# Where three pieces of VectorE and TensorE work stand in the second MLP halves of an mLSTM and Fourier-mixing kernel

## The chip, the cores and the metric

One core of a Trainium2 chip runs the whole kernel. The metric is the time of one execution on the device, in microseconds; smaller is better. Five engines run side by side, each through its own stream of instructions in the order in which the program was built: TensorE (PE in the profile, with its weight loads as PEld), VectorE (DVE), ScalarE (ACT), GpSimd (POOL) and SyncE (SP, which only issues transfers here). Products of PE land in the banks of PSUM and are read from there by DVE and ACT.

## The reference

For four batches, an mLSTM cell over 768 tokens and 8 heads of 40 gives x (768 tokens, 320 columns). Then:

```python
X = np.fft.fft(x, axis=1)
X = np.fft.fft(X, axis=2)
mixed = np.real(X).astype(np.float32)
u = x + mixed
mu = np.mean(u, axis=-1, keepdims=True)
var = np.mean((u - mu) ** 2, axis=-1, keepdims=True)
un = (u - mu) / np.sqrt(var + 1e-06)
ch = np.maximum(un @ w_ch1, 0.0) @ w_ch2
return (u + ch).astype(np.float32)
```

`w_ch1` is 320 x 1280 and `w_ch2` is 1280 x 320. Everything here is in fp32.

## The kernel before

**Stages.** Each batch goes through the mLSTM (in chunks of 128 tokens), the mixing (two Fourier transforms as products with tables, `mix_*`), the first MLP half (`mlp_block`, 1280 intermediate columns in ten blocks) and the second half (`mlp_out` for batch 0, `mlp_out_pair` for the others). The stages of different batches overlap: while the second half of batch b runs, the mixing of batch b + 1 is done, and beside batch 1's second half the mLSTM of batch 3 runs as well (beside batch 2's none is left).

**The order** is written out by hand. `at(slot, phase, fn, ...)` (L127) notes a call, and `run` (L130) makes all calls sorted by slot, then phase. The phases are `EVAC, FILL, MAIN, FILL_PE = range(4)` (L136), with fractions between: in a slot, 2.05 stands behind 2.0 and ahead of 2.5 and 2.6. The order of the calls is the order on every engine; nothing is moved later.

**The second half** (`plan_mlp`, L1352; `mlp_out_pair`, L1309). Six token columns of 128 are taken as three pairs n = 0, 1, 2, each with one column of either group. A pair is done by seven products in place of eight, in Strassen's manner: sums S1 to S4 of blocks of the intermediate columns (`hidden_sums`, L1300, one DVE instruction of 128x640 each, line L1307 in the profile; S4 is the tile `s_last`) meet sums T2 to T4 of the weights. Each product is ten matmuls of 160 columns (L1321) into one of two PSUM banks, and each is followed by a `residual` (L1267, instruction at L1271), in which DVE adds the scaled bank to the output column. A pair takes four slots, its steps:

- step 0: two products of plain blocks into banks x and y (four fifths of the first, two fifths of the second, the rest of the first, the rest of the second), and two residuals;
- step 1: S2 with T2 into x, S1 with a weight block into y, and two residuals;
- step 2: S3 with T3 into x, S4 with a weight block into y, two residuals and a store;
- step 3: one plain block with T4 into x, one residual and a store.

Banks x and y change places from one pair to the next. So step 0's first product of a pair needs the bank read by the second residual of step 2 of the pair before, and step 0's second product needs the bank read by its step 3 residual. Within a pair, step 1's first product waits for step 0's first residual, and step 2's first product for step 1's first residual. The sums of the next pair are made in steps 2 (S1, S2) and 3 (S3, S4).

**The mixing beside it** (`plan_mix`, L1062). For batches 2 and 3 it lies in the slots s_mix + 0 to s_mix + 11, which are the twelve slots of batch 1's and batch 2's second half: s_mix + 4 is step 0 of pair 1, s_mix + 8 is step 0 of pair 2. `mix_feat` (L965, L986) multiplies with the feature table into a bank `pu`: 128x161, 128x159 and 128x320, for p = 0, 1, 2. p = 1 and p = 2 use the same bank. `mix_add` (L988) adds `pu` to a token column on DVE: L1008 to L1011 and the statistics L1013 and L1014; for column 4 a copy and a memset (L1003, L1004) come first. The columns are added in the order 0, 5, 1, 4, 2, 3, in the slots s_mix + 4, 4, 5, 6, 8, 9, at phase MAIN + 0.5; columns 2 and 3 read the product p = 2. ScalarE centres a column (L1022, `uc`), PE transposes it (L1033), and ScalarE copies it to `uT` (L1038).

**`mlp_sums`** (L1178, L1183) makes four differences of `uT` on DVE (128x384 each: T3, B12, T2, T4) that the first MLP half of the next batch uses; its first product at step 1 reads B12, and its step 2 uses the bank of the last `residual` of the second half before.

Of the kernel before, what the change touches and what calls it, by code (L numbers as in the profile page):

```python
# [30 lines left out]
TG = NT // 2  # L31
# [26 lines left out]
def kernel(  # L58
# [68 lines left out]
    def at(slot, phase, fn, *args):  # L127
        plan.setdefault((slot, phase), []).append((fn, args))
# [7 lines left out]
    EVAC, FILL, MAIN, FILL_PE = range(4)  # L136
# [925 lines left out]
    def plan_mix(b, s0, x_done, s_feat, s_add, s_turn):  # L1062
        for j in range(TG):
            p = TG - 1 - j
            if b == 0:
                at((17, 18, 18.5)[j], FILL + (0.1, 0.07, 0.3)[j], mix_fold, b, p)
                s, phase = ((17, 3), (19, 3), (22, 4))[j]
                for i, part in enumerate(((0,), (1,)) if j == 1 else ((0, 1),)):
                    at(s, FILL_PE + phase + 0.1 * i, mix_seq, b, p, part)
                at(*((18, FILL_PE + 0.2) if j == 0 else (s, FILL_PE + phase + 0.2)), mix_tail, b, p)  # L1070
            else:
                at(x_done[j] + (b > 1 and j == TG - 1), FILL + 0.5 if b < 2 else FILL_PE + 0.2, mix_fold, b, p)
            if b > 0 and j == 0:
                for step in range(2):
                    at(*((x_done[-1], FILL + 0.55) if b == 1 else (x_done[-1] + 2 + 2 * step, FILL_PE + 0.25)),
                       mix_fold_again, b, step)
                at(s0, FILL_PE + 4, mix_seq, b, p, (0,))
                at(s0 + 1, FILL_PE + 4, mix_seq, b, p, (1,))
                at(s0 + 2, FILL_PE + 4, mix_tail, b, p)
        for i in range(2):  # L1080
            at(s0 + 1 if b == 0 else s0 + 1 + i, FILL, mix_seq_out, b, i)
        at(s0 + (1 if b == 0 else 3), FILL + 0.1, mix_tail_out, b)
        for p in range(TG):
            for i in range(3) if b == 0 and p == TG - 1 else ():
                at(s_feat[p] + i, FILL_PE + 5.1, mix_feat, b, p, slice(i, i + 1))
            if b == 0 and p == TG - 2:
                at(s_feat[p], FILL_PE + 4.06, mix_feat, b, p, slice(0, 3))
                at(s_feat[p] + 3, FILL_PE + 5.05, mix_feat, b, p, slice(3, 5))
            elif b == 0 and p == 0:
                at(s_feat[p], FILL_PE + 4, mix_feat, b, p, slice(0, 2))  # L1090
                at(s_feat[p], FILL_PE + 4.04, mix_feat, b, p, slice(2, 3))
            elif b > 0 or p < TG - 1:
                at(s_feat[p], FILL_PE + 4, mix_feat, b, p)
        for c, a, t in zip(ORDER, s_add, s_turn):
            at(a, FILL if b < 2 else MAIN + 0.5, mix_add, b, c)
            at(*(((32, EVAC + 0.1) if c == 3 else (a, FILL + 0.25) if c in (4, 2) else (t, FILL + 0.1)) if b == 0 else
                 (t, FILL + 0.1)), mix_center, b, c)
            at(t, FILL_PE + (5 if b == 0 or c in ORDER[:4] else -0.1), mix_turn, b, c)
            if b > 0:
                at(t, FILL_PE + 6, mix_turn_out, b, c)  # L1100
            elif t < s_mlp:
                at(t + 1, FILL + 0.2, mix_turn_out, b, c)
            else:
                at(t + 1, EVAC, mix_turn_out, b, c)
# [247 lines left out]
    def plan_mlp(b, s):  # L1352
        groups = range(NT // TG)
        for i in range(NFF // 2) if b > 0 else ():
            for step in range(4):
                at(s, MAIN, mlp_block, b, i, step)
                s += 1
            end = i == NFF // 2 - 1
            for n, (gr, f) in enumerate(((1, 2 * i + 1), (1, 2 * i), (0, 2 * i))):
                at(*((s - 1, MAIN + (-0.1 if gr else 0.1)) if end else (s + n, MAIN + 0.5)), mlp_relu_in_place, gr, f)  # L1360
        for gr, n in IN_ORDER if b == 0 else ():
            for f in (2 * n, 2 * n + 1):
                at(s, MAIN, mlp_in, b, gr, f)
                s += 1
            i = IN_ORDER.index((gr, n))
            if i < 4 or i % 2 == 0:
                at(*((s, MAIN + 0.5) if i == 1 else (s - 1, MAIN + (-0.1 if i == 2 else 0.2))), mlp_in_rests, b, i, False)
                if i > 3:
                    at(s - 1, MAIN + 0.25, mlp_in_rests, b, i + 1, True)
            for f in (2 * n, 2 * n + 1):  # L1370
                at(s + (i == 1), EVAC, mlp_relu, b, gr, f)
        if b > 0:
            for j in range(1, 5):
                at(s - (5, 4, 3, 3)[j - 1], FILL_PE + 0.3, hidden_sums, 0, (j,), 0, NFF // 2 - 2)
            at(s, EVAC, hidden_sums, 0, (1, 2), NFF // 2 - 2, NFF // 2)
            at(s, MAIN + 0.1, hidden_sums, 0, (3, 4), NFF // 2 - 2, NFF // 2)
        for n in range(TG) if b > 0 else ():
            for step in range(4):
                at(s, MAIN, mlp_out_pair, b, n, step)
                if n < TG - 1 and step > 1:  # L1380
                    for j in (2 * step - 3, 2 * step - 2):
                        at(s, MAIN + 0.6, hidden_sums, n + 1, (j,))
                s += 1
        for gr in groups if b == 0 else ():
            for i in range(TG):
                for half in range(2):
                    at(s, MAIN, mlp_out, b, gr, i, half)
                    s += 1
                n = gr * TG + i
                at(*((s + 2, MAIN + 0.1) if n == 0 else (s + 1, EVAC) if n == 1 else (s, EVAC)), mlp_store, b, gr, i)  # L1390
# [11 lines left out]
    def plan_batch(b, s_mlstm, s_mix, s_mlp):  # L1402
        if b == 0:
            plan_mlstm(b)
        else:
            plan_halves(b, s_mlstm)
        done = [s_mlstm + n for n in ((17, 19, 22) if b == 0 else (14, 17, 20))]
        assert s_mix >= done[-1] and s_mlp >= s_mix + 9
        late = [s_mlp + 2 * c for c in range(TG)]
        if b == 0:  # L1410
            feat = [s_mix + 1, s_mix + 1, s_mix + 2]
            turn = [s_mix + 2, s_mix + 3, s_mix + 4]
            add = turn + [s_mix + 5, s_mix + 6, s_mix + 7]
            late = [s_mlp, s_mlp + 1, s_mlp + 2]
        else:
            feat = [s_mix + c for c in ((3, 4, 6) if b == 1 else (3, 4, 7))]
            add = [s_mix + c for c in ((4, 4, 5, 6, 7, 7) if b == 1 else (4, 4, 5, 6, 8, 9))]
            turn = [s_mix + c for c in ((5, 6, 6) if b == 1 else (6, 7, 8))]
            late = [s_mix + c for c in ((7, 8, 8) if b == 1 else (9, 10, 10))]
            at(s_mlp, EVAC + 0.5, mlp_sums)  # L1420
        plan_mix(b, s_mix, done, feat, add, turn + late)
        s = s_mlp + NFF + 2
        at(s, FILL + 0.6, mix_rstd, b)
        for n in range(3):
            at(48 + n if b == 0 else s, FILL + 0.65, mix_rstd_step, b)
        plan_mlp(b, s_mlp)

    s_mlp = 31
    plan_batch(0, 0, 22, s_mlp)
    plan_batch(1, 32, 54, s_mlp + MLP_SLOTS)  # L1430
    plan_batch(2, 54, 83, s_mlp + 2 * MLP_SLOTS)
    plan_batch(3, 86, 115, s_mlp + 3 * MLP_SLOTS)
    for n in range(4):
# [181 lines left out]
```

## Time and profile before

| | us |
|---|---|
| median of 3 runs | 393.28 |
| lowest, highest | 390.28, 393.6 |
| the profiled execution | 390.56 |
| its span, first to last instruction | 388.8 |
| second half of batch 1, with the mixing of batch 2 | 197.7 to 244.1 |
| second half of batch 2, with the mixing of batch 3 | 284.4 to 324.2 |

The profile gives the busy time of each engine, and for each instruction that found its engine idle the wait and what ended it. A row of the timeline is: start in us from the first instruction, duration in us, engine, line of the kernel, operation, output<-inputs, shape, count, and in brackets the idle time ahead of it with its releaser. Ends of matmuls are modelled, so a row's duration overlaps the next row's start; the distance from start to start is the pace of PE. The token columns of all batches are named x in the trace; which batch is meant follows from the place.

### The profile page before, as it was taken

What the parts mean: (1) busy time and instruction counts of PE and PEld (TensorE: products, weight loads), DVE (VectorE), ACT (ScalarE), POOL (GpSimd) and SP (SyncE); (2) the same over time, 40 slices, a digit from 0 to 9 for tenths busy, and PEclk for the clock granted to TensorE, in tenths of its full rate; (3) what the DMA queues carried; (4) which work ended last, traced back from release to release, by engine and by line L of the source; (5) the groups of instructions that cost most, each with busy time, mean ns of one, the idle gap of its engine ahead of it and who ended that gap; (6) DMA issues with size and microseconds to landing.
All of it is one profiled execution on the core that took longest, in us unless ns stands there. A gap on an engine that the chain in (4) does not pass through costs nothing.

```text
span 388.8 us, 11401 instructions
## 1 busy us (share of the span) xinstructions
PE 375.2 (96%) x4598; PEld 274.1 (70%) x4598; DVE 282.4 (73%) x668; ACT 175.4 (45%) x505; POOL 132.3 (34%) x238
## 2 busy tenths in 40 slices
PE   8999888999999999999999999999999999999996
PEld 6887455666567777565578989565588996546996
DVE  8798898799997596786965786876755785246651
ACT  5988766868342233654553052663530133545000
POOL 5665434866685122561601433651300000020000
PEclk9999999999999999999999999999999999999999
DMA  7979489699971243464003644700001000000010
GB/s 203 293 211 322 134 232 265 177 276 260 233 191 36 88 140 110 143 179 121 0 3 90 155 117 114 195 21 3 0 0 35 5 31 34 2 0 2 35 35 34
DMA packets 21617, 43.99 MB, mean 113 GB/s; under 512 B 3493, under 2 KB 9853, under 8 KB 21437
## 3 DMA queue, kind: packets, MB, share of 16 engines
q1 hardware_dynamic: 21564, 43.27, 38.7%
q8 instruction: 36, 0.59, 0.7%
q14 instruction: 17, 0.13, 0.1%
HBM read 39.16 MB, written 4.10 MB: 111 GB/s over the span
## 4 chain that ended last, share of the span: by engine, by line
PE 74%; DVE 17%; issue 3%; ACT 1%; POOL 0%; DVEq 0%; ACTq 0%; POOLq 0%
PE po L1321 21%; PE pm L1195 16%; PE po L1265 8%; PE pm L1112 7%; PE pm L1129 4%; PE ph L581 4%; PE ps L581 4%; PE pu L986 3%; DVE so L771 2%; PE pz L940 2%; DVE x L758 1%; PE hb L581 1%; PE put L1033 1%; PE pzt L940 1%; DVE fe L878 1%
## 5 line engine op out<-in xcount | busy, mean ns | idle before, releaser
L1271 DVE SCALAR_TENSOR_TENSOR x<-po,rstd,x 128x160 f32<-128x160 f32 (+1 forms) x69 | 27.2, 394 | 38.3 <-PE po L1321 35.9
L1201 DVE TENSOR_TENSOR h<-h,pm 128x384 f32<-128x384 f32 x60 | 30.5, 550 | 27.0 <-PE pm L1112 12.6
L577 POOL TENSOR_SCALAR_AFFINE_SELECT W<-W 64x512 f32<-64x512 f32 x36 | 28.3, 786 | 32.5 <-ACT W L550 31.2
L704 POOL TENSOR_TENSOR C<-C,decB 128x164 f32<-128x164 f32 x33 | 18.4, 559 | 59.4 <-DVE C L711 58.0
L1195 PE MATMUL pm<-uT,w_sb 128*128 128x384 f32 x90 | 37.8, 507 | 0.4 <-DVE uT L1183 0.2
L550 ACT ACTIVATE W<-W,colT 128x64 f32<-128x64 f32 x144 | 36.7, 337 | 0.0
L1265 PE MATMUL po<-w_sb,h 128*128 128x320 f32 x120 | 33.9, 433 | 0.0
L1112 PE MATMUL pm<-uT,w_sb 64*64 64x384 f32 x320 | 33.3, 497 | 0.0
L1057 POOL TENSOR_TENSOR t<-rstd 128x6 f32<-128x6 f32 x12 | 3.5, 292 | 80.4 <-DVE v L1051 79.9
L562 POOL TENSOR_TENSOR qg<-qk,Gb 128x512 f32<-128x512 f32 x21 | 27.0, 1284 | 10.5 <-DMA qk<-in_qkT 10.2
L1321 PE MATMUL po<-T,S 128*128 128x160 f32 x180 | 27.9, 302 | 1.1 <-DVE x L1271 1.1
L1265 PEld LDWEIGHTS po<-w_sb,h 128*128 128x128 f32 x120 | 22.4, 190 | 9.1 <-issue 0.3
L1129 PE MATMUL pm<-uT,w_sb 128*128 128x384 f32 x80 | 28.5, 496 | 0.0
L1321 PEld LDWEIGHTS po<-T,S 128*128 128x128 f32 x180 | 25.4, 190 | 2.4 <-DVE x L1271 1.5
L1321 PE MATMUL po<-w_sb,h 128*128 128x160 f32 x180 | 26.3, 300 | 0.0
L1321 PEld LDWEIGHTS po<-w_sb,h 128*128 128x128 f32 x180 | 25.2, 190 | 1.5 <-DVE x L1271 0.3
L1195 PEld LDWEIGHTS pm<-uT,w_sb 128*128 128x128 f32 x90 | 15.4, 189 | 14.7 <-DVE h L1201 6.7
L1248 ACT ACTIVATE h<-h 128x384 f32<-128x384 f32 x45 | 23.1, 520 | 2.9 <-DVE h L1201 2.9
L1112 PEld LDWEIGHTS pm<-uT,w_sb 64*64 64x64 f32 x320 | 11.3, 132 | 18.1 <-issue 14.9
L1022 ACT ACTIVATE uc<-x 128x384 f32<-128x384 f32 x24 | 14.5, 615 | 19.9 <-DVE x L1014 19.9
L1038 ACT COPY uT<-put 128x384 f32<-128x384 f32 x21 | 9.6, 478 | 26.9 <-PE put L1033 26.8
L568 POOL TENSOR_TENSOR vw<-kvt,colT 128x328 f32<-128x328 f32 x23 | 20.0, 869 | 4.0 <-issue 2.2
(255 smaller groups left out, 833.2 us busy)
## 6 DMA issues: line engine op xcount, KB each, us to landing
kvt<-in_kv SPq DMA_DIRECT2D x24, 336.0 KB
qk<-in_qkT SPq DMA_DIRECT2D x48, 160.0 KB
raw<-in_w SPq DMA_DIRECT2D x10, 640.0 KB
Gb<-G_d SPq DMA_DIRECT2D x42, 128.0 KB
W<-M_d SPq DMA_DIRECT2D x36, 128.0 KB
so<-in_o SPq DMA_DIRECT2D x24, 160.0 KB
out<-x SPq DMA_DIRECT2D x24, 160.0 KB
ds_sb<-in_dft_s SPq DMA_DIRECT2D x1, 1158.0 KB
```

Of the source, the lines that this page charges most:

```text
L550: nc.scalar.activation(out=k.W[:, h, :], in_=M, func=AF.Exp, scale=-1.0, bias=colT[:, c, 0, b * H + h:b * H + h + 1])
L562: nc.gpsimd.tensor_tensor(out=k.qg[:, :, t], in0=k.qk[:, 0, :, t], in1=k.Gb[:, :, t], op=OP.mult)
L577: nc.gpsimd.affine_select(out=W, in_=W, compare_op=OP.is_ge, fill=0.0, base=base, pattern=[[0, H], [-1 if back else 1, LH]], channel_multi ...
L581: nc.tensor.matmul(out, w, x, start=start, stop=True, skip_group_check=True)
L1112: nc.tensor.matmul(banks[i][half(cols)], w1_rest(n)[half(i), half(cols)], u[half(i)], start=start, stop=not start, skip_group_check=True)
L1129: nc.tensor.matmul(k.pm[i], w1_block(ch, f // 2 * 2 + i), u[2 * ch], start=(ch == 0 and not ahead), stop=(ch == 1 and (ahead or n == 2)), ...
L1195: nc.tensor.matmul(bank, w, u, start=start, stop=True, skip_group_check=True)
L1201: nc.vector.tensor_tensor(out=h, in0=h, in1=bank, op=OP.add)
L1248: nc.scalar.activation(out=h, in_=h, func=AF.Relu, scale=-1.0)
L1265: nc.tensor.matmul(k.po[m], hidden(gr, f)[:, i * L:(i + 1) * L], w2_sb[:, f, :], start=(f == 0), stop=(f == NFF - 1))
L1271: nc.vector.scalar_tensor_tensor(out=u, in0=po, scalar=k.rstd[:, c:c + 1], in1=u, op0=OP.mult, op1=OP.add)
L1321: nc.tensor.matmul(po, a[:, f], w[:, f], start=start and f == 0, stop=f == half - 1, skip_group_check=True)
```

## The change

Three calls are put at other places; no instruction is added, removed or altered.

- `hidden_sums` for the next pair: S3 and S4 go from the slot of step 3 to the slot after it, that is step 0 of the next pair, at the same phase MAIN + 0.6. S1 and S2 stay. This concerns batches 1, 2 and 3, pairs 1 and 2.
- `mix_feat` with p = 2, for batches 2 and 3: from slot s_mix + 7, phase FILL_PE + 4 (behind step 3 of pair 1) to slot s_mix + 8, phase MAIN + 0.05 (behind the products of step 0 of pair 2).
- `mlp_sums` for batches 2 and 3: from the first slot of the next first half to the slot before it, phase MAIN - 0.05, that is ahead of step 3 of pair 2 with its residual. Batch 1 keeps its place.

```diff
@@ plan_mix
             elif b == 0 and p == 0:
                 at(s_feat[p], FILL_PE + 4, mix_feat, b, p, slice(0, 2))
                 at(s_feat[p], FILL_PE + 4.04, mix_feat, b, p, slice(2, 3))
+            elif b > 1 and p == TG - 1:
+                at(s_feat[p] + 1, MAIN + 0.05, mix_feat, b, p)
             elif b > 0 or p < TG - 1:
                 at(s_feat[p], FILL_PE + 4, mix_feat, b, p)
@@ plan_mlp
                 at(s, MAIN, mlp_out_pair, b, n, step)
                 if n < TG - 1 and step > 1:
                     for j in (2 * step - 3, 2 * step - 2):
-                        at(s, MAIN + 0.6, hidden_sums, n + 1, (j,))
+                        at(s + 1 if j > 2 else s, MAIN + 0.6, hidden_sums, n + 1, (j,))
                 s += 1
@@ plan_batch
-            at(s_mlp, EVAC + 0.5, mlp_sums)
+            at(*((s_mlp, EVAC + 0.5) if b == 1 else (s_mlp - 1, MAIN - 0.05)), mlp_sums)
```

In the built streams the change moves instructions on two engines: on DVE the sums, the adds around them and the four differences, on PE the three products of `mix_feat`. The streams of ACT, POOL and SP are the same as before.

## The prediction

> **What bounds the kernel now.** The page first: TensorE (PE) is busy 96% of the span at the full granted clock, so only its own idle time can be won and whatever makes it wait costs in full.
>
> ```profile
> span 388.8 us, 11401 instructions
> ...
> PE 375.2 (96%) x4598; PEld 274.1 (70%) x4598; DVE 282.4 (73%) x668; ACT 175.4 (45%) x505; POOL 132.3 (34%) x238
> ...
> PEclk9999999999999999999999999999999999999999
> ```
>
> Next the waits of PE between 198 and 327 us, which hold the output halves of batches 1 and 2 (197.7 to 244.1 and 284.4 to 324.2; batch 3's ends the span). All three name VectorE (DVE):
>
> ```profile
> PE po L1321 <- DVE x L1271: 1.1, 1, 1.1
> PE pu L986 <- DVE x L1011: 0.4, 1, 0.4
> PE pm L1195 <- DVE uT L1183: 0.2, 1, 0.2
> ```
>
> Then the timeline there (start us, us, engine, line). Batch 1, pairs 1 and 2:
>
> ```profile
> 212.48 0.81 DVE L1307 TENSOR_TENSOR S<-h,h 128x640 f32<-128x640 f32 x1
> 213.21 0.82 DVE L1307 TENSOR_TENSOR s_last<-h,S 128x640 f32<-128x640 f32 x1
> ...
> 216.43 0.39 DVE L1271 SCALAR_TENSOR_TENSOR x<-po,rstd,x 128x160 f32<-128x160 f32 x1 [1.57 <-PE po L1321]
> ...
> 220.85 0.29 DVE L711 TENSOR_TENSOR C<-C,ps 128x164 f32<-128x164 f32 x1
> 221.06 0.38 DVE L1271 SCALAR_TENSOR_TENSOR x<-po,rstd,x 128x160 f32<-128x160 f32 x1
> ...
> 221.49 1.63 PE L1321 MATMUL po<-T,S 128*128 128x160 f32 x10
> ...
> 233.30 0.87 DVE L1271 SCALAR_TENSOR_TENSOR x<-po,rstd,x 128x160 f32<-128x160 f32 x2
> ...
> 233.73 1.62 PE L1321 MATMUL po<-T,S 128*128 128x160 f32 x10 [1.08 <-DVE x L1271]
> ```
>
> Batch 2, the same places, and its hand-off to batch 3's first half:
>
> ```profile
> 306.25 0.35 DVE L1271 SCALAR_TENSOR_TENSOR x<-po,rstd,x 128x160 f32<-128x160 f32 x1
> ...
> 306.79 1.52 PE L1321 MATMUL po<-T,S 128*128 128x160 f32 x10
> ...
> 311.80 0.78 PE L986 MATMUL pu<-dd_sb,Z 128*128 128x161 f32 x4 [0.44 <-DVE x L1011]
> ...
> 313.89 0.38 DVE L1271 SCALAR_TENSOR_TENSOR x<-po,rstd,x 128x160 f32<-128x160 f32 x1
> ...
> 325.86 0.91 PE L1195 MATMUL pm<-uT,w_sb 128*128 128x384 f32 x2 [0.24 <-DVE uT L1183]
> ```
>
> See in it: pair 1's S3 and S4 (212.48, 213.21) stand ahead of a 1.57 us hole in DVE: free. From 217 on DVE runs two token adds back to back, and the residual that frees PE's bank ends at 221.44, 0.05 before PE restarts; in batch 2 it ends 306.60, 0.19 before. There DVE has nothing to spare.
>
> **Units from rows.** Ten 160-column matmuls (one product) take 1.36 (379.93 to 381.29), the feature product 1.09 (228.03 to 229.12), three transposes 0.33 (309.51 to 309.84), a 384-column matmul 0.32 (324.16 to 325.45 for four). A restart after a wait costs 0.10 more (221.49 to 222.95 is 1.46). On DVE, start to next start: S3 0.73, S4 0.73, S1 with S2 1.58, residual 0.30, token add 1.66, column 4's add 2.31, one `mlp_sums` subtraction 0.59. A residual starts 0.20 after its product; PE follows 0.05 after a residual.
>
> **Part 1: S3, S4 of the next pair one slot later.** Six moves, two DVE instructions each; no DMA, and the built streams of PE, ACT, POOL and SP keep their order here. They leave the place before step 0's residuals and come behind them, but at phase 2.6, that is behind the token adds at 2.5, and ahead of step 1's residuals.
>
> *Pair 1, batch 1.* The adds still start at 217.54, since they follow a residual that PE paces. S3 starts at 220.85, S4 at 221.58, L711 at 222.31, step 1's first residual at 222.52 instead of 221.06; PE restarts at 222.95 instead of 221.49: +1.46. Queued behind the sums: both residuals of step 1, the add of column 1, all that follows. *Pair 1, batch 2.* The residual goes from 306.25 to 307.71, PE from 306.79 to about 308.13, plus a restart: +1.43. Bounds: the hole they leave gives nothing back (DVE waits there for PE), so no gain; lower 1.26 (1.46 less the 0.19 of slack) per batch, upper 1.96 (two at 0.98, the slowest row of these sums); I take the 0.73 pitch, since POOL does nothing there in batch 2 and little in batch 1.
>
> *Batch 3, no adds between.* S3 and S4 make step 0's first residual late twice now (PE resumes at 368.64 and 378.47 with 0.13 lost each). Behind step 0 they start at 378.9, step 1's residual ends 380.8, PE needs it at 381.2: hidden, slack 0.4. -0.26.
>
> **Part 2: feature product p=2 behind step 0 of pair 2** (with pair 2's S3, S4 behind the add of column 2). Now it stands between step 3 and step 0 of pair 2, and its 1.09 us cover a DVE chain: last residual of step 2, add of column 4, S1, S2, then step 3's residual, which frees the bank of step 0's second product.
>
> *Batch 1.* PE's step 2 ends at 224.41; that residual ends 229.91, and PE gets to the product at 230.53: slack 0.62. Without the feature product PE comes 1.09 earlier and waits 0.52 with the latency, +0.10. In exchange S3, S4 no longer stand (231.58 to 233.07) ahead of step 0's first residual: transposes at 232.16 end 232.49 but PE went on at 233.73; 1.24 and a restart go, -1.34. The later sums start after the column 2 add and are done before PE, busy 2.7 us with attention products, wants step 1's residual. Sum: 0.62 - 1.34 = -0.72.
>
> *Batch 2.* No attention work lies between. The stall at 311.80 goes (0.60 past the pace, as the product before began at 309.84; with 0.08 and 0.05 of slow matmuls behind it, 0.73), but PE then meets the bank at 312.62 on the old clock, while the chain frees it at 314.32 as before: step 0 still ends at 316.05, and the 1.09 now come on top. Then the product, add of column 2 (317.34), S3 (319.00), S4 (319.73), step 1's residual ending 320.84: PE, ready for step 2 at 320.52, waits 0.37, +0.10. Sum: 1.09 + 0.47 = +1.56. If the add starts earlier (no row shows it for this product), 0 to 0.47 of that falls away.
>
> **Part 3: `mlp_sums` ahead of the last residual** (batches 2 and 3; four subtractions). They wait for ScalarE's last uT copy, and behind them queue the last residual, its store, and the bank of the next half's step 2. Batch 2 to 3: copy ends 323.53, B12 is ready at 324.75, PE wants it at 325.45: the 0.41 and 0.10 of the 325.86 stall go, -0.51; the residual ends 326.3, its bank is wanted at 326.7. Batch 1 to 2: PE does not wait there and attention work covers it: 0.
>
> In that hand-off T2's subtraction (245.94) ran 0.89 inside a GpSimd select (245.46 to 247.34), against 0.56 in batch 2: stretched, not blocked. The Trainium skill, "SBUF — State Buffer", section "SBUF: two separate sides", calls the port pair of the two engines an exclusive lock for a whole instruction; by that T2 would start after the select and the last residual would come 0.1 late at its bank (248.76), the sum 0.1 higher. The trace disagrees.
>
> **Sum.** Batch 1: 1.46 - 0.72 = +0.74. Batch 2: 1.43 + 1.56 - 0.51 = +2.48. Batch 3: -0.26. Together +3.0 us, 0.76%. The profiled execution took 390.56 (span 388.8); its sum is 393.5. The median of the runs is 393.28, 0.7% above it (lowest 390.28); on the median it is 396.2, which I forecast: 396.2 us.
>
> **Rivals.**
> *A, faster: the stalls go and no new one comes.* That needs PE to have slack at 221.49 and 306.79. It would win 1.34, 0.73, 0.51, 0.26 and 0.1 at 221.49: 2.9, giving 390.3. For it: the six stalls are real. Against: the 0.05 and 0.19 above, with 1.46 put in. It decides where the two token adds end more than 1.4 earlier than now. Chance 0.08.
> *B, dearer: DVE's delay goes on through ScalarE to the transposes.* In my working, column 5's transposes find their centred input 0.16 early in both batches, batch 2's last ones 0.2 early. Once that slack is gone, each wait costs about 0.4, and with sums at 0.98 instead of 0.73 (+1.0) the total is +4 to +5.2: 398 with the likeliest. Chance 0.25.
> *C, half clock.* The new waits (1.4 to 1.7 us) are longer than the old. The window 230 to 240 us holds the 1.08 wait at a granted 1.00, so the trace speaks against it. If one product after each of five waits ran at half the pitch, 5 x 1.36 = 6.8 would come on top: 403. Chance 0.02. The Trainium skill, "TensorE: Matmul & The Clock Gate", section "A second HAM failure mode: psum-queue depth-cycling", says that PE idling briefly between groups of matmuls can make the clock swing; no row here shows it.
> *D, it nets to nothing* (losses of pair 1 met by gains, feature product still hidden in batch 2): 393.3. Chance 0.05. That the change does not do what it says is excluded: the built DVE and PE streams show each move.
>
> **Numbers.** The forecast has 0.60. Two runs of this kernel differ by 0.8%, so about 1% (3.9 us) can be told from no change. Its own range is +1.8 (without the 0.47 and 0.62) to +4.0 (slow sums). The range goes from 391.8, which is +1.5 on the lowest run before and takes in D, to 398.4, +5.1 on the median: it leaves out C, most of A and B's top. Over 1% slower: 0.17 of B, 0.02 of C, 0.10 of the forecast: 0.29. Over 1% faster: 0.04, of A and of noise. Within 1%: 0.67.
>
> **What would show it.** In the profile after: the wait of PE on L1271 grows from one of 1.1 to several between 1 and 2 us, at the start of step 2 of pair 1 in batches 1 and 2, each behind S3 and S4; step 0's second product of pair 2 waits on step 3's residual; the L986 and L1183 waits vanish; batch 3's product cadence is unbroken at step 1. I am wrong if DVE's token adds in pair 1 end earlier, or if PE shows no wait at pair 1's step 2.

## The result and the profile after

| | before | after |
|---|---|---|
| median of 20 runs each, taken side by side, us | 392.79 | 397.03 |
| lowest, highest | 389.46, 397.38 | 394.15, 403.35 |
| the profiled execution | 390.56 | 398.33 |
| its span | 388.8 | 396.6 |

The changed kernel is slower: the ratio is 1.0117, with a 95% interval of 1.0091 to 1.0144. The same kernel measured again, in another set of runs, gave 395.22 against 393.12, a ratio of 1.0068 (1.0027 to 1.0109). The medians are of all runs, the ratios of the fast ones alone: a few executions of either kernel run in a slower state. Where the two kernels' work differs, the traces say it more sharply than whole runs can. The table gives the time between fixed points of the trace: from the first output product of a half (0.3 us behind the times given ahead for the halves) to the first product of the next first half, and from there to the next output product ("first half"); the last stretch ends where the last residual starts.

| stretch, us | before | after | after, measured again |
|---|---|---|---|
| start of batch 1's second half | 198.05 | 202.40 | 199.61 |
| second half of batch 1 | 46.06 | 46.80 | 46.81 |
| first half of batch 2 | 40.60 | 41.03 | 40.77 |
| second half of batch 2 | 39.45 | 42.47 | 42.44 |
| first half of batch 3 | 31.88 | 31.36 | 31.35 |
| second half of batch 3 | 29.53 | 29.26 | 29.26 |
| all five | 187.52 | 190.91 | 190.63 |

So the change costs 3.4 us in the one profile and 3.1 in the other. The first row is not its work: the instructions up to there are the same, and this start lay between 197.38 and 202.40 in the twelve profiles of this study.

The page of the changed kernel, the same three lines as before:

```profile
span 396.6 us, 11399 instructions
...
PE 378.1 (95%) x4598; PEld 275.3 (69%) x4598; DVE 282.5 (71%) x668; ACT 174.9 (44%) x505; POOL 132.1 (33%) x238
...
PEclk9999999998999999999999999999999999999999
```

The one 8 in the clock row is in the part that the change doesn't touch; it comes again at the end. The waits of TensorE between 195 and 340 us:

```profile
PE po L1323 <- DVE x L1273: 4.7, 5, 1.5
```

Three different small waits of 1.7 us together have become five of one kind, 4.7 us, all of an output product (now L1323) for a residual (now L1273). The waits at the feature product and at the differences are gone, and so is the one of 1.08 at 233.73. The timeline of the changed kernel shows each of the five, first batch 1, pairs 1 and 2:

```profile
225.20 0.79 DVE L1309 TENSOR_TENSOR S<-h,h 128x640 f32<-128x640 f32 x1
225.91 0.82 DVE L1309 TENSOR_TENSOR s_last<-h,S 128x640 f32<-128x640 f32 x1
...
226.88 0.67 DVE L1273 SCALAR_TENSOR_TENSOR x<-po,rstd,x 128x160 f32<-128x160 f32 x2
...
227.31 1.63 PE L1323 MATMUL po<-T,S 128*128 128x160 f32 x10 [1.41 <-DVE x L1273]
...
235.34 0.38 DVE L1273 SCALAR_TENSOR_TENSOR x<-po,rstd,x 128x160 f32<-128x160 f32 x1
...
235.78 1.90 PE L1323 MATMUL po<-w_sb,h 128*128 128x160 f32 x12 [0.34 <-DVE x L1273]
```

S3 and S4 (225.20, 225.91) now stand between the token adds and step 1's residuals. Both residuals could have run earlier (two in one row, back to back), and TensorE waits 1.41 us for the first of them. Some eight us later, with no feature product in between, step 0's second product waits 0.34 us for step 3's residual. Batch 2, the same places:

```profile
311.78 0.79 DVE L1309 TENSOR_TENSOR S<-h,h 128x640 f32<-128x640 f32 x1
312.49 0.82 DVE L1309 TENSOR_TENSOR s_last<-h,S 128x640 f32<-128x640 f32 x1
313.22 0.67 DVE L1273 SCALAR_TENSOR_TENSOR x<-po,rstd,x 128x160 f32<-128x160 f32 x2
...
313.66 1.62 PE L1323 MATMUL po<-T,S 128*128 128x160 f32 x10 [1.18 <-DVE x L1273]
...
320.85 0.38 DVE L1273 SCALAR_TENSOR_TENSOR x<-po,rstd,x 128x160 f32<-128x160 f32 x1
...
321.28 1.90 PE L1323 MATMUL po<-w_sb,h 128*128 128x160 f32 x12 [1.54 <-DVE x L1273]
...
324.30 0.32 DVE L1008 TENSOR_TENSOR x<-x,pu 128x161 f32<-128x161 f32 x1 [0.70 <-PE pu L986]
...
327.86 1.63 PE L1323 MATMUL po<-T,S 128*128 128x160 f32 x10 [0.22 <-DVE x L1273]
```

The largest is at 321.28: step 3's residual comes when it came before but for the delay of pair 1 (30.62 us after the half's start in place of 29.18), behind the add of column 4 and the two sums S1 and S2. TensorE gets there earlier, because the 1.09 us of feature product that stood there are now done later.

The numbers in brackets count from the modelled end of the last matmul, which lies behind its true pace, so they make a wait look shorter than it is. From start to start the new delays of pair 2 are larger: at 235.78, eight matmuls of 0.136 us from 234.18 are done at 235.27, so TensorE stands for 0.51 us; at 321.28, from 318.49, for 1.70; at 327.86, 2.07 us after the product before in place of 1.69 in the kernel before, for 0.38.

### The profile page after: what moved, and what is told of

It is laid out like the page before. It is cut to its first block, busy times and chain, and to the rows that moved or that the text cites. A ratio compares the mean times of both kernels' runs of the same rounds, so it can differ in the third digit from the quotient of the medians.

```text
span 396.6 us, 11399 instructions
## 1 busy us (share of the span) xinstructions
PE 378.1 (95%) x4598; PEld 275.3 (69%) x4598; DVE 282.5 (71%) x668; ACT 174.9 (44%) x505; POOL 132.1 (33%) x238
## 4 chain that ended last, share of the span: by engine, by line
PE 74%; DVE 14%; DMA 3%; issue 3%; ACT 1%; POOL 0%; DVEq 0%; ACTq 0%; SPq 0%
PE po L1323 19%; PE pm L1197 16%; PE po L1267 8%; PE pm L1114 7%; PE pm L1131 7%; PE ph L581 4%; PE ps L581 4%; PE pu L986 2%; PE pz L940 2%; PE hb L581 1%; DVE so L771 1%; PE pzt L940 1%; DMA raw<-in_w 1%; DVE S L1309 1%; DMA Gb<-G_d 1%
## 5 line engine op out<-in xcount | busy, mean ns | idle before, releaser
L1273 DVE SCALAR_TENSOR_TENSOR x<-po,rstd,x 128x160 f32<-128x160 f32 (+1 forms) x69 | 26.9, 394 | 38.4 <-PE po L1323 36.0
L1203 DVE TENSOR_TENSOR h<-h,pm 128x384 f32<-128x384 f32 x60 | 30.5, 549 | 27.9 <-PE pm L1114 12.6
L1197 PE MATMUL pm<-uT,w_sb 128*128 128x384 f32 x90 | 37.5, 506 | 0.1
L1114 PE MATMUL pm<-uT,w_sb 64*64 64x384 f32 x320 | 34.5, 498 | 0.5 <-issue 0.5
L562 POOL TENSOR_TENSOR qg<-qk,Gb 128x512 f32<-128x512 f32 x21 | 26.9, 1282 | 11.2 <-PE put L1033 10.5
L1323 PE MATMUL po<-T,S 128*128 128x160 f32 x180 | 27.8, 301 | 2.8 <-DVE x L1273 2.8
L1131 PE MATMUL pm<-uT,w_sb 128*128 128x384 f32 x80 | 30.2, 520 | 0.0
L1323 PE MATMUL po<-w_sb,h 128*128 128x160 f32 x180 | 26.8, 301 | 1.9 <-DVE x L1273 1.9
L1323 PEld LDWEIGHTS po<-T,S 128*128 128x128 f32 x180 | 25.4, 190 | 4.2 <-DVE x L1273 3.5
L1323 PEld LDWEIGHTS po<-w_sb,h 128*128 128x128 f32 x180 | 25.3, 190 | 3.8 <-DVE x L1273 2.7
L1197 PEld LDWEIGHTS pm<-uT,w_sb 128*128 128x128 f32 x90 | 15.5, 189 | 14.0 <-DVE h L1203 6.7
L1131 PEld LDWEIGHTS pm<-uT,w_sb 128*128 128x128 f32 x80 | 15.0, 199 | 10.5 <-issue 2.9
```

Source lines behind the costliest of these rows:

```text
L562: nc.gpsimd.tensor_tensor(out=k.qg[:, :, t], in0=k.qk[:, 0, :, t], in1=k.Gb[:, :, t], op=OP.mult)
L1114: nc.tensor.matmul(banks[i][half(cols)], w1_rest(n)[half(i), half(cols)], u[half(i)], start=start, stop=not start, skip_group_check=True)
L1131: nc.tensor.matmul(k.pm[i], w1_block(ch, f // 2 * 2 + i), u[2 * ch], start=(ch == 0 and not ahead), stop=(ch == 1 and (ahead or n == 2)), ...
L1197: nc.tensor.matmul(bank, w, u, start=start, stop=True, skip_group_check=True)
L1203: nc.vector.tensor_tensor(out=h, in0=h, in1=bank, op=OP.add)
L1273: nc.vector.scalar_tensor_tensor(out=u, in0=po, scalar=k.rstd[:, c:c + 1], in1=u, op0=OP.mult, op1=OP.add)
```

## The experiments

Ten more runs were made: nine other kernels, and the changed kernel once more. The main reading is the stretches above; the time of a whole run is given only where it was repeated. A "half" below is a second half.

**One part alone: the sums.** Before, with only this:

```diff
-                        at(s, MAIN + 0.6, hidden_sums, n + 1, (j,))
+                        at(s + 1 if j > 2 else s, MAIN + 0.6, hidden_sums, n + 1, (j,))
```

> The change with part 1 alone (S3 and S4 a slot later; feature product and differences at their old places). Measured in the profile as five stretches, from the first output matmul of a half to the first matmul of the next stage: before, batch 1's second half takes 46.06 us, batch 2's 39.45, batch 3's first half 31.88 and batch 3's second half to its last residual 29.53; in the changed kernel 46.80, 42.47, 31.36 and 29.26. Theory (residuals queue behind sums and adds on VectorE): pair 1 costs 1.46 and 1.43, pair 2 wins 1.34 in batch 1 and loses 0.8 in batch 2, batch 3 wins 0.26: 46.2, 41.7, 31.9, 29.3, together +2.1 on before. Rival (pair 1 is hidden and the feature product makes the loss): no wait at step 2 of pair 1, 44.7, 39.5, 31.9, 29.3, together -1.6.

Measured: the halves take 46.20, 41.66 and 29.25. TensorE waits 1.41 at step 2 of pair 1 of batch 1 and 1.17 in batch 2, the same two waits as after the whole change. The sums alone explain them.

**One part alone: the feature product.** The change with the sums and the differences put back:

```diff
-                        at(s + 1 if j > 2 else s, MAIN + 0.6, hidden_sums, n + 1, (j,))
+                        at(s, MAIN + 0.6, hidden_sums, n + 1, (j,))
...
-            at(*((s_mlp, EVAC + 0.5) if b == 1 else (s_mlp - 1, MAIN - 0.05)), mlp_sums)
+            at(s_mlp, EVAC + 0.5, mlp_sums)
```

> Part 2 alone (the third feature product behind step 0 of pair 2, sums and differences at their old places). Theory: nothing in batch 1, where step 0's first residual stays behind S3 and S4 and sets step 1 as before (46.1); in batch 2 the product's 1.09 us no longer run under the VectorE chain (40.5); 31.9 and 29.5. Together +1.1. Rival (the feature product makes most of the loss): +3 or more, in both batches.

Measured: batch 2's half takes 40.53 as expected, batch 1's 46.50, which is 0.44 more than before, where nothing had been expected. The timeline shows where it comes from: S4, ahead of the residual that TensorE waits for, takes 1.26 us in place of 0.82. Its neighbours on the two engines, each instruction in a row of its own:

```profile
232.73 0.83 DVE L1309 TENSOR_TENSOR S<-h,h 128x640 f32<-128x640 f32 x1
232.84 1.24 POOL L577 TENSOR_SCALAR_AFFINE_SELECT W<-W 64x512 f32<-64x512 f32 x1
...
233.49 1.26 DVE L1309 TENSOR_TENSOR s_last<-h,S 128x640 f32<-128x640 f32 x1
...
234.14 1.13 POOL L577 TENSOR_SCALAR_AFFINE_SELECT W<-W 64x512 f32<-64x512 f32 x1
```

Taken alone, a select needs 0.65 (the shortest of the 36 before) and S4 0.82. Subtract these from the four ends (233.56, 234.08, 234.75, 235.27) and the works begin at 232.73, 233.43, 233.93 and 234.62: each starts some 0.14 before the end of the one ahead of it on the other engine. So, by this working, the two engines took turns, instruction by instruction; the time that an instruction is held off is shown as its own duration, not as idle time before it.

**One part alone: the differences.** Before, with only this:

```diff
-            at(s_mlp, EVAC + 0.5, mlp_sums)
+            at(*((s_mlp, EVAC + 0.5) if b == 1 else (s_mlp - 1, MAIN - 0.05)), mlp_sums)
```

> Part 3 alone (the four differences of token columns ahead of the last residual for batches 2 and 3). Theory: batch 3's first half loses its wait at the start, 31.88 to 31.4; the other stretches as before, together -0.5. Rival (the last residual comes late at its bank and gives it back): 31.9 or more, with a wait at the third product pair of the half.

Measured: batch 3's first half takes 31.35 (0.53 won), batch 2's 40.82 (0.22 lost). The win is the one expected; the loss is not, and is taken up below.

**The sums of pair 1 put back.** The change, with

```diff
-                        at(s + 1 if j > 2 else s, MAIN + 0.6, hidden_sums, n + 1, (j,))
+                        at(s + 1 if j > 2 and (n == 1 or b == 3) else s, MAIN + 0.6, hidden_sums, n + 1, (j,))
```

> The changed kernel with pair 1's S3 and S4 put back to step 3's slot in batches 1 and 2 alone. Theory: the waits at step 2 of pair 1 go, 1.46 in batch 1 and 1.43 in batch 2: 45.3, 41.0, 31.4, 29.3, together 0.5 over before. Rival (VectorE is simply full there, so its backlog only moves): under half of the 2.9 comes back, and step 0 of pair 2 waits longer than the 0.5 and 1.7 of the changed kernel.

Measured: 45.32 and 41.00. Against the changed kernel that is 1.48 and 1.47 less, the price of pair 1's sums in each batch; against the kernel before it is -0.74 and +1.55, which is what pair 2's part of the change does.

**Half the dose.** Before, with S4 of pair 1 alone a slot later:

```diff
-                        at(s, MAIN + 0.6, hidden_sums, n + 1, (j,))
+                        at(s + 1 if j == 4 and n == 0 and b < 3 else s, MAIN + 0.6, hidden_sums, n + 1, (j,))
```

> The kernel before, with S4 of pair 1 alone a slot later in batches 1 and 2: half the dose of the sums, nothing else changed. Theory (each sum ahead of step 1's residual costs its 0.73 of VectorE): step 2 of pair 1 waits 0.73 longer in batch 1, and 0.7 in batch 2 (0.73 less 0.14 of slack, and a restart of 0.1): 46.8, 40.6, 40.1, 31.9, 29.5, together +1.4. Rival (PE waits for the data of S3 and S4, not for the residual behind them): S3 is early now and S4 is wanted a product later, so no wait: +0.

Measured: 46.79 and 40.16, that is +0.73 and +0.71 for one instruction. Its place in the timeline:

```profile
221.34 0.79 DVE L1307 TENSOR_TENSOR s_last<-h,S 128x640 f32<-128x640 f32 x1
...
222.29 0.67 DVE L1271 SCALAR_TENSOR_TENSOR x<-po,rstd,x 128x160 f32<-128x160 f32 x2
...
222.72 1.49 PE L1321 MATMUL po<-T,S 128*128 128x160 f32 x9 [0.68 <-DVE x L1271]
```

The residual ahead of TensorE is late by one sum's pitch, and the time goes up by that pitch. So the price is the place in VectorE's queue, not the readiness of S3 or S4: with S3 long done and S4 early enough for step 2's second product, it's still paid.

**A token add moved out of the way.** The changed kernel, with the second add of pair 1 (column 5) a slot later:

```diff
-            add = [s_mix + c for c in ((4, 4, 5, 6, 7, 7) if b == 1 else (4, 4, 5, 6, 8, 9))]
+            add = [s_mix + c for c in ((4, 4, 5, 6, 7, 7) if b == 1 else (4, 5, 5, 6, 8, 9))]
```

> The changed kernel with column 5's token add one slot later, so that in pair 1 one add, S3 and S4 stand ahead of step 1's residuals in place of two adds, S3 and S4. Stretches as in the runs before (changed kernel: 46.8, 41.0, 42.5, 31.4, 29.3). Theory that VectorE has no hole between pair 1's step 0 and pair 2's step 0, so that 1.46 us of sums cost there wherever they stand: the wait at step 2 of pair 1 goes (1.46 and 1.43), but step 3's residual of that pair comes later, PE waits there and at pair 2's step 0 instead, and at most 0.4 is won in each of the two halves: 46.5 and 42.2. Rival (it is only the place ahead of step 1's residuals that costs): the waits go and nothing takes their place, 45.3 and 41.0.

Measured: 46.27 and 42.15, 0.53 and 0.32 less than the changed kernel. The waits at step 2 of pair 1 are gone, but here is step 0 of pair 2 in batch 1:

```profile
231.71 1.49 PE L1323 MATMUL po<-w_sb,h 128*128 128x160 f32 x9 [1.46 <-DVE x L1273]
```

The wait has moved some eight us down the same queue (32.9 us after the half's start in place of 24.9). In batch 2 it stands at step 3 of pair 1, with 1.01 us. In this stretch VectorE has no hole into which 1.66 us of add or 1.46 us of sums would fit: in the kernel before it is idle there for 1.4 of 15.8 us (217.5 to 233.3), never for more than 0.61 at a time.

**The loss in batch 2's first half.** It is there in every kernel in which batch 2's differences stand ahead of the last residual (40.77 to 41.09 in six profiles) and in none of the others (40.59 to 40.61 in six). Before, the stores on SyncE's queue, the loads behind them and what hangs on these loads:

```profile
242.70 2.51 SPq L1274 DMA_DIRECT2D out<-x  x2
245.27 0.75 SPq L517 DMA_DIRECT2D qk<-in_qkT  x2
...
249.43 1.08 SPq L537 DMA_DIRECT2D Gb<-G_d  x2
...
256.58 1.27 POOL L562 TENSOR_TENSOR qg<-qk,Gb 128x512 f32<-128x512 f32 x1
257.30 0.91 DVE L771 SCALAR_TENSOR_TENSOR so<-so,den 128x320 f32<-128x320 f32 x1
258.88 0.55 DVE L1201 TENSOR_TENSOR h<-h,pm 128x384 f32<-128x384 f32 x1
259.44 0.89 PEld L1112 LDWEIGHTS pm<-uT,w_sb 64*64 64x64 f32 x16 [0.55 <-issue]
```

The changed kernel, 5.1 us later in time:

```profile
247.79 5.42 SPq L1276 DMA_DIRECT2D out<-x  x2
253.26 0.75 SPq L517 DMA_DIRECT2D qk<-in_qkT  x2
...
256.39 1.08 SPq L537 DMA_DIRECT2D Gb<-G_d  x2
...
262.11 1.27 POOL L562 TENSOR_TENSOR qg<-qk,Gb 128x512 f32<-128x512 f32 x1 [0.48 <-DMA so<-in_o]
262.31 1.43 DVE L771 SCALAR_TENSOR_TENSOR so<-so,den 128x320 f32<-128x320 f32 x1
264.40 0.55 DVE L1203 TENSOR_TENSOR h<-h,pm 128x384 f32<-128x384 f32 x1
...
265.00 0.52 PEld L1114 LDWEIGHTS pm<-uT,w_sb 64*64 64x64 f32 x11 [0.37 <-DVE h L1203]
```

The second store of the first row waits at the head of SyncE's queue for the last residual, now behind four subtractions: 2.51 us become 5.42. The loads of the last mLSTM chunk are issued behind it: against the half's start, the first (qk) 2.9 us later, those of Gb 1.9. So GpSimd's product (L562), which reads qk and Gb, waits 0.48 us for a load. The profile names that of so as the one that landed last; which load held it is not shown. VectorE's L771, which needs 0.49 alone, is held off by L562 until 263.25 and ends at 263.74. The add at L1203 is 0.44 late against the half's start, and TensorE's next products wait 0.37 us for it. The wait is on the row of the weight loads, since part of the block's products had started and TensorE itself was not idle: that is why the list of TensorE's waits does not show it. Three more profiles have the same order of instructions and other waits at L562: 0.21 (the changed kernel again), 0.27 (the differences alone) and 0.28 us (column 5's add later). Their losses are 0.17, 0.22 and 0.23, so loss and wait go together.

This was tested by leaving batch 2's differences where they were, in the changed kernel:

```diff
-            at(*((s_mlp, EVAC + 0.5) if b == 1 else (s_mlp - 1, MAIN - 0.05)), mlp_sums)
+            at(*((s_mlp, EVAC + 0.5) if b < 3 else (s_mlp - 1, MAIN - 0.05)), mlp_sums)
```

> The changed kernel with the differences of batch 2 back behind the last residual, nothing else. Theory (the late store holds back SyncE's queue): 46.8, 40.6, 42.5, 31.4, 29.3, and the loads behind that store are issued about 3 us earlier against the first matmul of batch 2's first half. Rival: 40.8 to 41.1 in the second stretch.

Measured: batch 2's first half takes 40.61, and the rest as in the changed kernel (46.80, 42.46, 31.35, 29.26). The same rows:

```profile
242.78 2.51 SPq L1276 DMA_DIRECT2D out<-x  x2
245.34 2.55 SPq L517 DMA_DIRECT2D qk<-in_qkT  x2
...
250.28 1.08 SPq L537 DMA_DIRECT2D Gb<-G_d  x2
...
256.66 1.27 POOL L562 TENSOR_TENSOR qg<-qk,Gb 128x512 f32<-128x512 f32 x1
257.37 0.90 DVE L771 SCALAR_TENSOR_TENSOR so<-so,den 128x320 f32<-128x320 f32 x1
258.95 0.55 DVE L1203 TENSOR_TENSOR h<-h,pm 128x384 f32<-128x384 f32 x1
```

The wait at L562 is gone, and the loss with it. Of the "about 3 us" only the first load has its full share (2.9); issuing the two qk loads takes longer here (2.55 us in place of 0.75, for a reason that was not looked into), so the loads of Gb are issued only 1.1 us earlier than in the changed kernel. That was enough.

**The change measured again**, with no edit, in five rounds (the second column of stretches above):

> The changed kernel once more. Theory: the halves account for 3.0 to 3.5 us (0.75 to 0.9%), and what the first measurement had above that lies in the first 200 us, whose instructions are the same in both kernels and which take 198 to 202 in the profiles so far: the stretches come again as 46.8, 40.8 to 41.1, 42.5, 31.4, 29.3, the first part takes another time than 202, and the ratio lies at 1.007 to 1.012. Rival (the change also costs about 1 us where no instruction of it stands): the first part takes 202 again and the ratio is 1.012 or more.

Measured: 46.81, 40.77, 42.44, 31.35, 29.26, the first part 199.61, the ratio 1.0068. The rival fell; 40.77 and 1.0068 lie a hair under the ranges of the theory.

**A version that takes the parts where VectorE has room.** Batches here are those whose second half runs. The sums of pair 1 stay in batches 1 and 2; in batch 1 pair 2's S3 and S4 go a slot later; in batch 2 it is pair 2's S1 and S2, behind the residual that freed the bank; batch 3 has all of them a slot later. The feature product beside batch 1's half keeps its old place, and the one beside batch 2's goes a little later in the same slot (in the code these are the mixings b == 2 and b == 3). The differences are as in the changed kernel.

```diff
-            elif b > 1 and p == TG - 1:
-                at(s_feat[p] + 1, MAIN + 0.05, mix_feat, b, p)
+            elif b == 3 and p == TG - 1:
+                at(s_feat[p], FILL_PE + 5.5, mix_feat, b, p)
...
-                        at(s + 1 if j > 2 else s, MAIN + 0.6, hidden_sums, n + 1, (j,))
+                        at(s + 1 if b == 3 or n == 1 and (j > 2) == (b == 1) else s, MAIN + 0.6, hidden_sums, n + 1, (j,))
```

> The parts that win, each where it wins: pair 1's sums as before in batches 1 and 2; pair 2's S3 and S4 a slot later in batch 1, its S1 and S2 behind step 3's residual in batch 2; in batch 3 all four sums a slot later; the third feature product at its old place in batch 1, in batch 2 behind column 5's transposes of the same slot; the differences ahead of the last residual. Theory: 44.7 (the wait of 1.3 goes), 40.6 to 41.0, 39.0 (a shorter VectorE chain into pair 2, 0.5), 31.4, 28.9 (0.6, no late bank at all): together 2.5 to 3.0 under before, a time 0.7% lower. Rival (VectorE's backlog only moves on, as the sums of pair 2 still lie in it): under 1 us won, a time within 0.3%.

Measured: 44.71, 41.09, 39.26, 31.35, 28.88, together 185.31, which is 2.21 less than before; the ratio is 0.9919 (0.9877 to 0.9961). That is under the 2.5 expected at the least: 39.26 for 39.0, and 41.09, the loss just explained. So the same with batch 2's differences in their old place too:

```diff
-            at(*((s_mlp, EVAC + 0.5) if b == 1 else (s_mlp - 1, MAIN - 0.05)), mlp_sums)
+            at(*((s_mlp, EVAC + 0.5) if b < 3 else (s_mlp - 1, MAIN - 0.05)), mlp_sums)
```

> The chosen parts, with the differences of batch 2 back behind the last residual (batch 3's stay ahead of it). Batch 2's first half took 40.6 in the kernels with the old place and 40.8 to 41.1 in those with the new one, which the prediction had put at nothing. Theory: the last store of batch 1's second half waits for its residual at the head of SyncE's queue, 3 us longer, and the loads of the last mLSTM chunk (qk, kvt, W, so, Gb) are issued behind it, so that GpSimd waits for Gb and PE for a mix input: at the old place 40.6 and no such wait; stretches 44.7, 40.6, 39.3, 31.4, 28.9, together 0.4 to 0.5 under the chosen kernel and 2.7 under before, a time 0.7% lower. Rival (the extra comes from VectorE and GpSimd meeting otherwise, whatever the place of the differences): 40.8 to 41.1 again.

Measured: 44.73, 40.60, 39.24, 31.35, 28.88, together 184.80, 2.72 less than before. The ratio is 0.9885 (0.9838 to 0.9933). From 195 to 345 us TensorE has no wait above 0.14 us left. This version beats the kernel before in whole runs and the changed one by its stretches (184.80 against 190.91).

## Why the prediction was right, and where it missed

| term | forecast, us | measured, us | from |
|---|---|---|---|
| pair 1's sums, batch 1 | +1.46 | +1.48 | 46.80 - 45.32 |
| pair 1's sums, batch 2 | +1.43 | +1.47 | 42.47 - 41.00 |
| pair 2, batch 1 | -0.72 | -0.74 | 45.32 - 46.06 |
| pair 2, batch 2 | +1.56 | +1.55 | 41.00 - 39.45 |
| differences, batch 2 to 3 | -0.51 | -0.53 | 31.35 - 31.88 |
| differences, batch 1 to 2 | 0 | +0.43 (again: +0.17; alone: +0.22) | 41.03 - 40.60 |
| sums of batch 3 | -0.26 | -0.27 | 29.26 - 29.53 |
| sum | +2.96 | +3.39 (again: +3.11) | |

**Part 1 and the main step were right.** The residual ended 0.05 and 0.19 us ahead of TensorE's restart at 221.49 and 306.79; by the prediction's own unit 0.05 of that is what TensorE takes to follow, so nothing and 0.14 were to spare. Two sums of 0.73 put ahead of the residual were paid in full. The half dose, at half the price, shows that the queue is what charges.

**Part 2 was right, and so was its split.** In batch 1 the stall of 1.08 goes and a smaller one comes; in batch 2 the feature product had covered a chain that still ends at the same time, so that its 1.09 us come on top. From start to start the three delays are 0.51, 1.70 and 0.38 us; the prediction worked out 0.52, 1.70 (312.62 to 314.32) and 0.37, so its sums did not come out by errors that cancel. The forecast left open whether the product's add starts at the end of the product; it does (324.30, 0.70 after VectorE had gone idle for it), and so nothing fell away.

**Part 3 failed at one step**: "Batch 1 to 2: PE does not wait there and attention work covers it: 0." The sentence ahead of it names the store among what queues behind the subtractions, but only TensorE's banks were followed from there. Behind that store stand the loads of the next chunk, on a queue that issues in order; the cover of attention work was itself waiting for those loads. The price was 0.17 to 0.49 over the six profiles. In the two at 0.49, pair 1's sums put back and the first of the chosen versions, L562 waits 0.8 and 0.9 us and runs behind L771 in place of ahead of it; TensorE is held a little further on, 0.7 us at the attention products (L581) in place of 0.14. The steps between are not worked out there. The Trainium skill, "DMA: Bandwidth & Descriptors", section "Anatomy of one DMA — SWDGE (gpsimd) path", says that a transfer's wait for a semaphore is spent on the issuing sequencer, before dispatch. That section is about transfers issued by GpSimd; these are issued by SyncE, and the trace agrees for them too: one late store, and the first load behind it 2.9 us later.

**A reading that was wrong, though it carried no term**: "stretched, not blocked". It took the row of two selects (245.46 to 247.34) for one instruction. In the timeline of the kernel before, looked at one by one, they are:

```profile
245.46 0.96 POOL L577 TENSOR_SCALAR_AFFINE_SELECT W<-W 64x512 f32<-64x512 f32 x1 [3.94 <-ACT W L550]
...
245.94 0.89 DVE L1183 TENSOR_TENSOR raw<-uT 128x384 f32<-128x384 f32 x1
246.48 0.86 POOL L577 TENSOR_SCALAR_AFFINE_SELECT W<-W 64x512 f32<-64x512 f32 x1
```

The first select ends at 246.42; the subtraction, 0.56 long by itself, ends at 246.82, so its work began at 246.26; the second select ends at 247.34 and began at 246.69. That is taking turns again. The Trainium skill, "SBUF — State Buffer", section "SBUF: two separate sides", has it so: a VectorE instruction with two SBUF inputs and a GpSimd instruction that reads SBUF exclude each other for their whole length. The trace agrees with it here, and so do the feature product's run (S4, +0.44) and L771 (+0.94); the prediction had read the opposite from the merged row.

**The rivals.** The faster one (A) fell: the old stalls do go, but there was no slack for the sums. B, the dearer one by transposes and ScalarE, fell: no wait of TensorE names a transpose's input, and S3 and S4 kept to 0.71 and 0.73 from start to start in place of 0.98. C fell: the windows of the changed kernel around the new waits show the full clock, the third number from the right in each row.

```profile
225.00:240.00 15.00, 13.25 (x208) 12.33 (x207) 13.14 (x41) 5.29 (x16) 4.82 (x8) 1.00 0.33 101
312.00:328.00 16.00, 13.06 (x93) 12.13 (x92) 12.47 (x35) 3.31 (x7) 0.00 (x0) 1.00 0.07 22
```

D fell with the sum. The signs that the prediction named came: three waits on L1273 between 1 and 2 us, two of them behind S3 and S4 at step 2 of pair 1 and one on step 3's residual, and none at the feature product or the differences. The forecast time, 396.2, lies between the two medians, 395.22 and 397.03; that the kernel would be over 1% slower was given 0.29, and the two ratios, 1.0117 and 1.0068, lie on either side of that bound. The first pair of medians differs by 4.24 us where its traces account for 3.39, the second pair by 2.10 where they account for 3.11. What is left over is of the size by which the first 200 us differ from one execution to the next, and was not taken apart further. So the closeness of the time itself is partly luck; it is the table of terms that bears the prediction out.

## What to carry to other kernels

Before work is moved later in an engine's queue, find the instruction behind it that frees something for the bounding engine, and compare its margin with the pitch of what is put ahead: at margins of 0.14 us and less, 1.46 us of sums cost 1.48 and 1.47, and moving the next thing on mostly moved the wait. When the delayed instruction has a transfer behind it, follow the queue of that transfer too: the loads behind a waiting store are late with it, whoever needs them. The same edit can win at one site and lose at another, so choose it site by site: taken only where they won, these moves and a few like them won 2.72 us in place of costing 3.4.

## What the runs showed of the hardware

An instruction of VectorE or GpSimd that was held off by the other engine showed no idle time for it here; its row just got longer: a select of 0.65 was shown as 1.24, S4 of 0.82 as 1.26, L771 of 0.49 as 1.43. So a row that is longer than others of the same shape may hold a wait; rows of two or more instructions have to be taken apart to see it.

The changed kernel's profile lost 4.6 us of the 7.8 in its span far ahead of the change, between 82 and 96 us (its matmuls lag those of before by 0.49 there at first and by 5.04 in the end). Its timeline and its windows there (the same columns as in the windows above):

```profile
83.85 1.00 PE L1114 MATMUL pm<-uT,w_sb 64*64 64x384 f32 x7 [0.50 <-issue]
...
90.18 0.44 PE L581 MATMUL ph<-kvt,W 64*64 64x41 f32 x14 [1.48 <-issue]
```

```profile
85.00:90.00 5.00, 3.71 (x120) 2.51 (x119) 3.79 (x6) 2.27 (x6) 2.36 (x4) 1.00 0.85 270
90.00:95.00 5.00, 4.82 (x23) 2.76 (x24) 3.06 (x12) 2.99 (x10) 1.95 (x4) 0.66 0.47 116
```

TensorE stood still for 1.48 us with nothing to wait for that the profile shows, and in the window behind it the granted clock was 0.66; before, the same windows have 1.00. The profile of the last chosen version has the same stop at the same place, 1.75 us at 90.26, and 0.66 behind it, so it is not of the changed kernel alone. The waits of 1.41 and 1.54 us above left the clock at 1.00. In seven more of the twelve profiles the clock row has a lower digit between 39 and 49 us, and the three without any reach batch 1's second half at 197.38 to 198.39, the others at 197.85 to 202.40. What held TensorE up at 90 us, and whether that stop lowered the clock, stays open. It does show that one profile against another is no measure of a change: the spans differ by 7.8 us, the work that the change touches by 3.4.
